# Moving the MLP's sums from VectorE to ScalarE and GpSimd, and fixing the order of the DMA and GpSimd queues

## Chip, core and metric

The kernel runs on one core of a Trainium2 chip. The metric is the device time in microseconds of one execution. The engines are called by the names that the profile uses: PE (TensorE; PEld is its weight load), DVE (VectorE), ACT (ScalarE), POOL (GpSimd) and SP (SyncE, which here only issues DMAs). Each engine takes its own instructions strictly in order; between engines an instruction waits for semaphores.

## What is computed

An attention block and a token-mixing MLP work on the same input and are mixed by a gate per token. S = 2048 tokens, D = 640 channels, H = 32 heads of 20, F = 1728, all float32:

```python
g = _sigmoid((x * gate_w).sum(-1, keepdims=True))
# a: attention
q, k, v = qkv[0], qkv[1], qkv[2]
scores = jnp.einsum("bhqd,bhkd->bhqk", q, k) * (Dh ** -0.5)
p = _softmax(scores, axis=-1)
o = jnp.einsum("bhqk,bhkd->bhqd", p, v)      # then @ wo
# b: MLP over the token axis
h = _layernorm(x, axis=-1)
u = _gelu(jnp.einsum("bsd,sf->bdf", h, w1) + b1)
y = jnp.einsum("bdf,fs->bds", u, w2) + b2    # transposed back
return g * a + (1 - g) * b
```

## The kernel before

**Precision.** Most products are made from numbers split into a high and a low part (`hi_lo`, L36): the high part is a rounded copy, the low part the difference. A product then takes three matmuls (high x high, high x low, low x high). In the MLP each matmul over 128 rows is cut in two halves of 64 rows that go to two accumulators side by side (`pair64`, L43); the two halves have to be summed afterwards. In this text they are `ps[0]` and `ps[1]`.

**Stages, in order of time.**

1. Projections (to about 220 us): units of q and k (`qk_unit`, L189) of 128 rows by 512 tokens, each of 15 matmuls, ACT writing the high part, DVE the low part, and SP storing both to q_d and k_d; v in between. In the last 24 units (L373) the first half of the channels is also normalised (`h_norm`, L314, POOL) and split (`h_split`, L318, ACT and POOL), the first four weight blocks are loaded (`w_raw`, L338) and split (`w_split`, L348), and the operands of the first pair of heads are loaded (`base_stack`, L114).
2. The MLP (about 220 to 745 us): `mlp` (L446) is a generator whose steps are one `pair64` each; 2592 steps. For each half d of the channels it makes 14 tiles u (48 steps each, one of them 32) and then 16 tiles y (40 steps each). Weights come in blocks of 128x512 (`w_need`, L364): loaded nine blocks ahead by SP, split four blocks ahead, high part on ACT, low part on POOL. A block feeds 12 steps, which are 24 matmuls.
3. Beside the MLP, scores: `s_tiles` (L136) makes a 128x512 tile of scores by one matmul and takes its row maxima by one DVE reduction (L148). The maxima of each query are needed later, to make the exponentials safe. 736 of the 2048 tiles are made here (S_AHEAD, L493), two at a time, spread evenly over the steps (L509); the others in the loop. After 64 tiles (half a pair of heads) the partial maxima are closed: a reduction, a negation, a split into high and low, a transposition (L151 to L157, all on DVE) and a store to m_d (L158).
4. The attention loop (about 745 to 1840 us): 16 pairs of heads times 32 iterations. An iteration makes four tiles of transposed scores (`st_op`, L640), four exponentials on ACT (L646), the four products with v for the iteration before (`pv_flush`, L580), and up to three of the remaining 1312 score tiles. The maxima enter the transposed scores as two extra rows of the operand (`load_m`, L120).
5. The output projection (from about 1840 us), which also adds the MLP's y, stored in between to y_d.

**Order.** PE's instructions run as the program lists them over the whole kernel, ACT's and DVE's from L212 to the end of the loop. POOL's and SP's are arranged by the scheduler of the framework, from its own estimates of durations, so a load may come earlier or later in its queue than the program has it. `settle` (L400) carries out evacuation steps a number of MLP steps after they were registered in `soon`.

**What the change touches.** `u_evac` (L408): ACT copies `ps[0]` to SBUF (L410), five steps later DVE adds `ps[1]` to it (L411), at step 10 follow gelu (L419) and the split. The tile FF has 64 rows in each half, so its two halves of rows are also swapped by DMAs and added on POOL (`u_swap`, L422). `y_evac` (L435): ACT scales and shifts `ps[0]` (L438), five steps later DVE adds the scaled `ps[1]` (L441) and SP stores the tile to y_d (L442). `h_norm` (L314) for the second half runs on POOL during the y tiles of the first half. `load_stack` (L96) issues 12 loads for a pair of heads on SP (14 with the rows of ones), for the first pair at unit 19, for pair p + 1 when pair p starts (`start_ahead`, L496); when pair 4 starts, the stack of the loop's first pair, its maxima and its v follow. The iteration of the loop takes its score tiles at L649 to L654.

Of the kernel before, what the change touches and what calls it, by code (L numbers as in the profile page):

```python
# [13 lines left out]
P = 128  # L14
# [14 lines left out]
def gated_mix(ctx, tc, xT, x, wqk, wv0, wv1, wo, w1, w1t, b1, w2, b2, out):  # L29
# [66 lines left out]
    def load_stack(p, ks, qs, full):  # L96
        for j in range(2):
            r0 = 64 * j
            h = 2 * p + j
            rows = slice(DH * h, DH * h + DH)  # L100
            kf = ks.bitcast(F32)
            nc.sync.dma_start(kf[r0: r0 + DH, :], k_d[0, rows, :])
            nc.sync.dma_start(kf[r0 + DH: r0 + 2 * DH, :], k_d[0, rows, :])
            nc.sync.dma_start(kf[r0 + 2 * DH: r0 + 3 * DH, :], k_d[1, rows, :])
            if full:
                nc.sync.dma_start(kf[r0 + 3 * DH: r0 + 3 * DH + 2, :], ones)
            for i in range(2):
                qf = qs[i].bitcast(F32)
                cols = slice(i * (S // 2), (i + 1) * (S // 2))
                nc.sync.dma_start(qf[r0: r0 + DH, :], q_d[0, rows, cols])  # L110
                nc.sync.dma_start(qf[r0 + DH: r0 + 2 * DH, :], q_d[1, rows, cols])
                nc.sync.dma_start(qf[r0 + 2 * DH: r0 + 3 * DH, :], q_d[0, rows, cols])

    def base_stack(p, full):  # L114
        ks = k8([P, S], F32R, f"ks{p}_{full}")
        qs = [q4([P, S // 2], F32R, f"qs{p}_{full}_{i}") for i in range(2)]
        load_stack(p, ks, qs, full)
        return ks, qs
# [16 lines left out]

    def s_tiles(p):  # L136
        for half in range(2):
            mx = cp.tile([P, 4, 2, 8], F32, tag="mx", bufs=2, name=f"mx{p}_{half}")
            for t in range(8):
                for kc in range(4):  # L140
                    for j in (1, 0):
                        def f(j=j, kc=kc, t=t):
                            ks, qs = s_src[p]
                            ps = s_tile([P, 512], f"s{p}_{half}_{t}_{j}_{kc}")
                            r = slice(64 * j, 64 * j + 3 * DH)
                            nc.tensor.matmul(ps, qs[half][r, t * P:(t + 1) * P], ks[r, kc * 512:(kc + 1) * 512],  # L146
                                             start=True, stop=True)
                            nc.vector.tensor_reduce(mx[:, kc, j, t: t + 1], ps, axis=AX.X, op=OP.max)  # L148
                        yield f
            mm = cp.tile([P, 16], F32, tag="mm", bufs=2, name=f"mm{p}_{half}")  # L150
            nc.vector.tensor_reduce(mm, mx.rearrange("p k j t -> p (j t) k"), axis=AX.X, op=OP.max)  # L151
            mc = cp.tile([P, 32], F32R, tag="mc", bufs=2, name=f"mc{p}_{half}")
            mt = cp.tile([P, 32], F32, tag="mt", bufs=2, name=f"mt{p}_{half}")
            nc.vector.tensor_scalar_mul(mc[:, :16], mm, -1.0)
            nc.vector.scalar_tensor_tensor(mc[:, 16:], mm, -1.0, mc[:, :16].bitcast(F32),
                                           op0=OP.mult, op1=OP.subtract)
            nc.vector.transpose(mt, mc.bitcast(F32))  # L157
            m_queue[0].dma_start(m_d[p, half], mt)  # L158
# [7 lines left out]
    m_queue = [nc.sync]  # L166
# [136 lines left out]

    hps = ExitStack()
# [9 lines left out]
    def h_norm(d, t):  # L314
        xm = xms[d, t]
        nc.gpsimd.tensor_scalar(xm, xm, negm[:, t:t + 1], rstd[:, t:t + 1], op0=OP.add, op1=OP.mult)
# [21 lines left out]
    def w_raw(k):  # L338
# [6 lines left out]
        nc.sync.dma_start(raw[:, :n, :m], src)  # L345
# [62 lines left out]
    def u_evac(f, d, ps, gh, gl):  # L408
        xg = gp.tile([P, HALF], F32, tag="xg", bufs=3, name=f"xg{d}_{f}")
        nc.scalar.activation(xg, ps[0], AF.Copy)  # L410
        soon.append([5, lambda: nc.vector.tensor_add(xg, ps[1], xg)])  # L411
# [10 lines left out]
    def u_swap(d, xg):  # L422
# [3 lines left out]
        nc.gpsimd.tensor_add(xg, xg, sw)  # L426
# [8 lines left out]
    def y_evac(t, d, ps):  # L435
        ty = hp.tile([P, HALF], F32, tag="ty", bufs=3, name=f"ty{d}_{t}")
        c = slice(t, t + 1)
        nc.scalar.activation(ty, ps[0], AF.Identity, bias=b2o[:, c], scale=omg[:, c])  # L438

        def rest():  # L440
            nc.vector.scalar_tensor_tensor(ty, ps[1], omg[:, c], ty, op0=OP.mult, op1=OP.add)  # L441
# [54 lines left out]
    def start_ahead(p):  # L496
        if 1 <= p + 1 < 6:
# [9 lines left out]
    for n, _ in enumerate(steps):  # L507
        settle()
        while done + 2 <= S_AHEAD and done < S_AHEAD * (n + 1) / STEPS:  # L509
            for _ in range(2):  # L510
                next(stream)()
            done += 2
    settle(True)
    while done < S_AHEAD:
        next(stream)()
# [19 lines left out]
    m_queue[0] = nc.gpsimd  # L535
# [85 lines left out]
    for p in range(NP):  # L621
# [3 lines left out]
        for it in range(32):  # L625
# [23 lines left out]
            due = min((p * 32 + it + 1) * LEFT // (NP * 32 - 38) + 1, LEFT)  # L649
            take = min(due - given, 3)  # L650
            for n in range(4):
                st_op((n + turn) % 2, n // 2, s_tile if n == 0 and take < 3 else st_tile)
                if n < take:
                    next(stream)()  # L654
            given += take
            if take and given == LEFT:
                next(stream, None)
# [83 lines left out]
```

## Time and profile before

| | us |
|---|---|
| median of 3 runs | 1918.32 |
| lowest and highest | 1918.08, 1920.92 |
| the profiled execution, whole | 1924.69 |
| its span in the profile | 1922.9 |

The profiled execution is another one than the three runs; it is 6.4 us above their median, and 1.8 us of it lie outside the span. Busy shares over the span are 98% for PE, 76% for DVE, 69% for ACT and 29% for POOL. They are averages over stages of quite different kinds, so the tables by stretch of time are read with them. A PE that is shown busy may still be slower than it could be, since ends of matmuls are modelled; the number of matmuls that start in a stretch is the surer measure. In a wait row stands the engine that waited, then the one that it waited for.

### The profile page before, as it was taken

The numbers are of one execution on the slowest core, as the hardware profiler recorded it, in microseconds if no ns is written. First come the engines' busy times: TensorE is split into PE (matmuls) and PEld (weight loads), VectorE is DVE, ScalarE is ACT, GpSimd is POOL, SyncE is SP. The second block draws the span as 40 slices with busy tenths as digits, with TensorE's granted clock in tenths as the row PEclk, the third lists the DMA queues.
The fourth block names the chain that finished last, engine by engine and source line by source line (L and its number), as shares of the span: only waits on it lengthen the run. The fifth ranks groups of instructions, "written<-read, shape, count | busy, mean of one in ns | idle before, by whom it ended". The sixth has DMA issues, their size and how long they took to land. (4 is left out here: it accounts for less than half of the span.)

```text
span 1922.9 us, 39183 instructions
## 1 busy us (share of the span) xinstructions
PE 1878.7 (98%) x14978; PEld 1162.0 (60%) x14978; DVE 1463.1 (76%) x2465; ACT 1335.4 (69%) x2595; POOL 557.5 (29%) x731
## 2 busy tenths in 40 slices
PE   9999889999999999999999999999999999999998
PEld 7998788998999996333333333333333333333378
DVE  4202388999999997888888888888888888886127
ACT  4253233343443335999999999999999999999930
POOL 1024266667776562210110101001220012111210
PEclk9999899999999998999999999999999999999999
DMA  8467775556655563315040404231542134211263
GB/s 282 139 198 220 208 180 153 148 162 175 171 141 142 163 177 93 80 40 113 7 97 12 99 16 89 53 84 24 107 101 69 32 76 99 48 34 52 70 217 134
DMA packets 153742, 216.63 MB, mean 113 GB/s; under 512 B 66783, under 2 KB 92991, under 8 KB 149647
## 3 DMA queue, kind: packets, MB, share of 16 engines
q1 hardware_dynamic: 136336, 186.96, 36.6%
q0 software_dynamic: 13472, 18.63, 4.3%
q10 hardware_dynamic: 3744, 8.52, 1.3%
q8 instruction: 118, 1.93, 0.5%
q14 instruction: 72, 0.58, 0.1%
HBM read 165.43 MB, written 48.25 MB: 111 GB/s over the span
## 5 line engine op out<-in xcount | busy, mean ns | idle before, releaser
L148 DVE TENSOR_REDUCE mx<-s 128x1 f32<-128x512 f32 x2048 | 1283.5, 683 | 168.8 <-PE s L146 149.5
L646 ACT ACTIVATE p<-st 128x512 f32<-128x512 f32 x2048 | 1050.8, 620 | 41.1 <-PE s L146 14.7
L643 PEld LDWEIGHTS st<-qs_True,ks_True 62*128 62x128 f32 x2048 | 326.5, 185 | 476.0 <-ACT p L646 229.8
L643 PE MATMUL st<-qs_True,ks_True 62*128 62x512 f32 x2048 | 606.5, 424 | 1.2 <-ACT p L646 0.8
L586 PE MATMUL pv<-p,v 128*32 128x512 f32 x4096 | 550.1, 606 | 0.0
L146 PE MATMUL s<-sk,sq 60*128 60x512 f32 x1280 | 442.2, 440 | 2.6 <-DVE mx L148 2.6
L41 POOL TENSOR_TENSOR wl<-wr,wh 128x512 fp32r<-128x512 f32 x228 | 271.8, 1215 | 117.4 <-ACT wh L38 100.2
L146 PE MATMUL s<-ks_False,qs_False 60*128 60x512 f32 x768 | 253.3, 411 | 11.7 <-DVE mx L148 11.7
L573 POOL DMA_DIRECT2D o_d<-oev x128 | 66.5, 519 | 611.4 <-DVE oev L567 593.3
L38 ACT ACTIVATE wh<-wr 128x512 fp32r<-128x512 f32 (+2 forms) x246 | 139.9, 594 | 137.0 <-PE y L46 50.4
L146 PEld LDWEIGHTS s<-sk,sq 60*128 60x128 f32 x1280 | 208.5, 184 | 21.6 <-DVE mx L148 12.7
L46 PE MATMUL y<-gh,wh 64*128 64x320 f32 x896 | 208.6, 310 | 0.0
L46 PE MATMUL u<-hh,wh 64*128 64x320 f32 x864 | 199.7, 310 | 4.4 <-ACT wh L38 4.4
L46 PE MATMUL y<-gh,wl 64*128 64x320 f32 x832 | 200.5, 310 | 2.7 <-POOL wl L41 2.7
L46 PE MATMUL y<-gl,wh 64*128 64x320 f32 x832 | 202.6, 310 | 0.0
L46 PE MATMUL u<-hl,wh 64*128 64x320 f32 x864 | 199.1, 309 | 0.0
L46 PE MATMUL u<-hh,wl 64*128 64x320 f32 x800 | 188.1, 311 | 4.5 <-POOL wl L41 4.5
L586 PEld LDWEIGHTS pv<-p,v 128*32 128x32 f32 x4096 | 83.0, 108 | 173.8 <-issue 162.1
L46 PEld LDWEIGHTS y<-gh,wh 64*128 64x128 f32 x896 | 154.3, 187 | 0.4
L146 PEld LDWEIGHTS s<-ks_False,qs_False 60*128 60x128 f32 x768 | 138.3, 188 | 24.9 <-DVE mx L148 23.4
L46 PEld LDWEIGHTS u<-hh,wh 64*128 64x128 f32 x864 | 150.0, 188 | 4.8 <-ACT wh L38 4.6
L46 PEld LDWEIGHTS u<-hl,wh 64*128 64x128 f32 x864 | 150.8, 188 | 0.3
(112 smaller groups left out, 1837.4 us busy)
## 6 DMA issues: line engine op xcount, KB each, us to landing
wr<-in_w_dram SPq DMA_DIRECT2D x200, 256.0 KB
qs_True<-q_d SPq DMA_DIRECT2D x192, 80.0 KB
ks_True<-k_d SPq DMA_DIRECT2D x96, 160.0 KB
sk<-k_d SPq DMA_DIRECT2D x60, 160.0 KB
sq<-q_d SPq DMA_DIRECT2D x120, 80.0 KB
qs_False<-q_d SPq DMA_DIRECT2D x72, 80.0 KB
ks_False<-k_d SPq DMA_DIRECT2D x36, 160.0 KB
v_d<-vt SPq DMA_DIRECT2D x32, 168.0 KB
```

Of the source, the lines that this page charges most:

```text
L38: nc.scalar.activation(hi, src, AF.Copy)
L41: (lo_eng or nc.vector).tensor_sub(lo, src, hi.bitcast(F32))
L46: nc.tensor.matmul(ps[k], a[r], b[r], start=start, stop=stop)
L146: nc.tensor.matmul(ps, qs[half][r, t * P:(t + 1) * P], ks[r, kc * 512:(kc + 1) * 512], start=True, stop=True)
L148: nc.vector.tensor_reduce(mx[:, kc, j, t: t + 1], ps, axis=AX.X, op=OP.max)
L573: nc.gpsimd.dma_start(o_d[DH * h: DH * h + DH, cols], ev[r: r + DH, :])
L586: nc.tensor.matmul(pv[r: r + 32, :], v_tiles[p][:, kt, 10 * j: 10 * j + 32], pts[j, c], start=(kt == 0), stop=(kt == NT - 1))
L643: nc.tensor.matmul(ps, ks[r, kt * P:(kt + 1) * P], qs[qh][r, c * 512:(c + 1) * 512], start=True, stop=True)
L646: nc.scalar.activation(pt, ps, AF.Exp, scale=SCALE)
```

## The change

Six things are altered.

- **Sums.** In `u_evac` and `y_evac` ACT now reads both accumulators (`half_sum`, a second copy, scaled for y), and POOL adds the two in SBUF six steps later. Gelu comes at step 18 instead of 10; the y tile's store is issued by ACT at step 24. The sum with the swapped halves comes at step 30 instead of at once. The normalisation of the second half of the channels (`h_norm`) is two ACT operations instead of one on POOL.
- **Maxima.** A closing is cut in three: the reduction on DVE two tiles after the last tile of a half, negation and split on POOL, and eight tiles later the transposition on DVE. The store goes to POOL's queue, in the MLP another eight tiles later.
- **Order.** POOL and SP run as programmed from L304 to the end of the loop.
- **Queues.** SP is left with loads. The first four weight blocks and the first stack are issued by POOL; the stack follows unit 19 instead of preceding it, and the first splits come one or two units later.
- **The second stack** is loaded when 48 score tiles have been made.
- **The loop.** In an iteration with two score tiles these follow its first and third tile of transposed scores instead of its first and second, and the order of the heads within it alternates differently. All score tiles are done six iterations earlier (44 instead of 38 before the end).

The diff, shortened:

```diff
-    def load_stack(p, ks, qs, full):
+    def load_stack(p, ks, qs, full, eng=nc.sync):
...
+    s_close = []
+
+    def s_max(p, half, mx):
+        mm = cp.tile([P, 16], F32, tag="mm", bufs=2, name=f"mm{p}_{half}")
+        mc = cp.tile([P, 32], F32R, tag="mc", bufs=2, name=f"mc{p}_{half}")
+        nc.vector.tensor_reduce(mm, mx.rearrange("p k j t -> p (j t) k"), axis=AX.X, op=OP.max)
+        nc.gpsimd.tensor_scalar_mul(mm, mm, -1.0)
+        hi_lo(mc[:, :16], mc[:, 16:], mm, hi_eng=nc.gpsimd, lo_eng=nc.gpsimd)
+        s_close.append([8, lambda: s_store(p, half, mc)])
+
+    def s_store(p, half, mc):
+        mt = cp.tile([P, 32], F32, tag="mt", bufs=2, name=f"mt{p}_{half}")
+        nc.vector.transpose(mt, mc.bitcast(F32))
+        s_close.append([M_LAG[0], lambda: m_queue[0].dma_start(m_d[p, half], mt)])
+
+    M_LAG = [8]
+
+    def s_next():
+        next(stream)()
+        for e in list(s_close):
+            e[0] -= 1
+            if e[0] <= 0:
+                s_close.remove(e)
+                e[1]()
...
-            mm = cp.tile([P, 16], F32, tag="mm", bufs=2, name=f"mm{p}_{half}")
-            nc.vector.tensor_reduce(mm, mx.rearrange("p k j t -> p (j t) k"), axis=AX.X, op=OP.max)
-            mc = cp.tile([P, 32], F32R, tag="mc", bufs=2, name=f"mc{p}_{half}")
-            mt = cp.tile([P, 32], F32, tag="mt", bufs=2, name=f"mt{p}_{half}")
-            nc.vector.tensor_scalar_mul(mc[:, :16], mm, -1.0)
-            nc.vector.scalar_tensor_tensor(mc[:, 16:], mm, -1.0, mc[:, :16].bitcast(F32),
-                                           op0=OP.mult, op1=OP.subtract)
-            nc.vector.transpose(mt, mc.bitcast(F32))
-            m_queue[0].dma_start(m_d[p, half], mt)
+            s_close.append([2, lambda p=p, half=half, mx=mx: s_max(p, half, mx)])
...
-    m_queue = [nc.sync]
+    m_queue = [nc.gpsimd]
...
+    ordered.enter_context(tc.manual_schedule(engines={EG.Pool, EG.SP}))
...
         xm = xms[d, t]
+        if d:
+            nc.scalar.activation(xm, xm, AF.Identity, bias=negm[:, t:t + 1])
+            nc.scalar.activation(xm, xm, AF.Copy, scale=rstd[:, t:t + 1])
+            return
         nc.gpsimd.tensor_scalar(xm, xm, negm[:, t:t + 1], rstd[:, t:t + 1], op0=OP.add, op1=OP.mult)
...
-        nc.sync.dma_start(raw[:, :n, :m], src)
+        (nc.gpsimd if k < AHEAD else nc.sync).dma_start(raw[:, :n, :m], src)
...
-        if n == 19:
-            s_src[0] = base_stack(0, False)
...
-        if n in (18, 19):
-            w_split(n - 18)
-            w_raw(n - 16)
+        if n in (19, 20):
+            w_split(n - 19)
+            w_raw(n - 17)
         qk_unit(m, w[m], q)
-        if n in (20, 21):
-            w_split(n - 18)
+        if n == 19:
+            s_src[0] = base_stack(0, False, nc.gpsimd)
+        if n in (22, 23):
+            w_split(n - 20)
...
         nc.scalar.activation(xg, ps[0], AF.Copy)
-        soon.append([5, lambda: nc.vector.tensor_add(xg, ps[1], xg)])
+        x2 = half_sum(ps[1], 1.0)
+        soon.append([6, lambda: nc.gpsimd.tensor_add(xg, xg, x2)])
         if f == FF:
-            soon.append([6, lambda: u_swap(d, xg)])
+            soon.append([7, lambda: u_swap(d, xg)])
+            soon.append([30, lambda: nc.gpsimd.tensor_add(xg, xg, sws.pop())])
             soon.append([44, lambda: u_tail(f, d, xg, gh)])
         else:
-            soon.append([10, lambda: u_gelu(f, xg, gh, gl)])
+            soon.append([18, lambda: u_gelu(f, xg, gh, gl)])
+
+    def half_sum(ps, scale):
+        x2 = gp.tile([P, HALF], F32, tag="x2", bufs=2, name="x2")
+        nc.scalar.activation(x2, ps, AF.Copy, scale=scale)
+        return x2
...
         nc.scalar.activation(ty, ps[0], AF.Identity, bias=b2o[:, c], scale=omg[:, c])
+        x2 = half_sum(ps[1], omg[:, c])
 
         def rest():
-            nc.vector.scalar_tensor_tensor(ty, ps[1], omg[:, c], ty, op0=OP.mult, op1=OP.add)
-            nc.sync.dma_start(y_d[t * P:(t + 1) * P, d * HALF:(d + 1) * HALF], ty)
-
-        soon.append([5, rest])
+            nc.gpsimd.tensor_add(ty, ty, x2)
+
+        def store():
+            nc.scalar.dma_start(y_d[t * P:(t + 1) * P, d * HALF:(d + 1) * HALF], ty)
+
+        soon.append([6, rest])
+        soon.append([24, store])
...
-        if 1 <= p + 1 < 6:
+        if 2 <= p + 1 < 6:
             s_src[p + 1] = base_stack(p + 1, False)
...
+            if done == 48:
+                s_src[1] = base_stack(1, False)
...
-    m_queue[0] = nc.gpsimd
+    M_LAG[0] = 0
...
-            due = min((p * 32 + it + 1) * LEFT // (NP * 32 - 38) + 1, LEFT)
+            due = min((p * 32 + it + 1) * LEFT // (NP * 32 - 44) + 1, LEFT)
             take = min(due - given, 3)
             for n in range(4):
-                st_op((n + turn) % 2, n // 2, s_tile if n == 0 and take < 3 else st_tile)
-                if n < take:
-                    next(stream)()
+                j = n // 2 if take == 2 else n % 2
+                st_op((j + turn) % 2, n % 2 if take == 2 else n // 2, s_tile if n == 0 and take < 3 else st_tile)
+                if n < take if take != 2 else n % 2 == 0:
+                    s_next()
```

More of the change, by code (lines that the diff above doesn't have):

```diff
@@ L101, in load_stack @@
             kf = ks.bitcast(F32)
-            nc.sync.dma_start(kf[r0: r0 + DH, :], k_d[0, rows, :])
-            nc.sync.dma_start(kf[r0 + DH: r0 + 2 * DH, :], k_d[0, rows, :])
-            nc.sync.dma_start(kf[r0 + 2 * DH: r0 + 3 * DH, :], k_d[1, rows, :])
+            eng.dma_start(kf[r0: r0 + DH, :], k_d[0, rows, :])
+            eng.dma_start(kf[r0 + DH: r0 + 2 * DH, :], k_d[0, rows, :])
+            eng.dma_start(kf[r0 + 2 * DH: r0 + 3 * DH, :], k_d[1, rows, :])
             if full:
-                nc.sync.dma_start(kf[r0 + 3 * DH: r0 + 3 * DH + 2, :], ones)
+                eng.dma_start(kf[r0 + 3 * DH: r0 + 3 * DH + 2, :], ones)
             for i in range(2):
@@ L109, in load_stack, with base_stack @@
                 cols = slice(i * (S // 2), (i + 1) * (S // 2))
[L110 to L114, printed above, removed]
+                eng.dma_start(qf[r0: r0 + DH, :], q_d[0, rows, cols])
+                eng.dma_start(qf[r0 + DH: r0 + 2 * DH, :], q_d[1, rows, cols])
+                eng.dma_start(qf[r0 + 2 * DH: r0 + 3 * DH, :], q_d[0, rows, cols])
+    def base_stack(p, full, eng=nc.sync):
         ks = k8([P, S], F32R, f"ks{p}_{full}")
         qs = [q4([P, S // 2], F32R, f"qs{p}_{full}_{i}") for i in range(2)]
-        load_stack(p, ks, qs, full)
+        load_stack(p, ks, qs, full, eng)
         return ks, qs
@@ L134, in load_v, with s_finish @@
         nc.sync.dma_start(v_tiles[p], v_d[p // 8, :, :, c0: c0 + NPAIR].rearrange("t p c -> p t c"))
+    s_close = []
[18 more added lines that the diff above has]
+                e[1]()
+    def s_finish():
+        next(stream, None)
+        while s_close:
+            s_close.pop(0)[1]()
     def s_tiles(p):
@@ L410, in u_evac @@
         nc.scalar.activation(xg, ps[0], AF.Copy)
-        soon.append([5, lambda: nc.vector.tensor_add(xg, ps[1], xg)])
+        x2 = half_sum(ps[1], 1.0)
+        soon.append([6, lambda: nc.gpsimd.tensor_add(xg, xg, x2)])
         if f == FF:
-            soon.append([6, lambda: u_swap(d, xg)])
+            soon.append([7, lambda: u_swap(d, xg)])
+            soon.append([30, lambda: nc.gpsimd.tensor_add(xg, xg, sws.pop())])
             soon.append([44, lambda: u_tail(f, d, xg, gh)])
         else:
-            soon.append([10, lambda: u_gelu(f, xg, gh, gl)])
+            soon.append([18, lambda: u_gelu(f, xg, gh, gl)])
[3 more added lines that the diff above has]
+        return x2
+    sws = []
     def u_gelu(f, xg, gh, gl):
@@ L425, in u_swap @@
         nc.gpsimd.dma_start(sw[TL:], xg[:TL])
-        nc.gpsimd.tensor_add(xg, xg, sw)
+        sws.append(sw)
     def u_tail(f, d, xg, gh):
@@ L514, in gated_mix @@
     while done < S_AHEAD:
-        next(stream)()
+        s_next()
         done += 1
@@ L647, in st_op @@
                 pts[j, c] = pt
-            due = min((p * 32 + it + 1) * LEFT // (NP * 32 - 38) + 1, LEFT)
+            due = min((p * 32 + it + 1) * LEFT // (NP * 32 - 44) + 1, LEFT)
             take = min(due - given, 3)
             for n in range(4):
-                st_op((n + turn) % 2, n // 2, s_tile if n == 0 and take < 3 else st_tile)
-                if n < take:
-                    next(stream)()
+                j = n // 2 if take == 2 else n % 2
+                st_op((j + turn) % 2, n % 2 if take == 2 else n // 2, s_tile if n == 0 and take < 3 else st_tile)
+                if n < take if take != 2 else n % 2 == 0:
+                    s_next()
             given += take
             if take and given == LEFT:
-                next(stream, None)
+                s_finish()
             turn = (turn + take) % 2
```

## The prediction

> **What bounds the kernel now.** I read the page's slices first, to find stages, and then the windows of the stage that the change touches.
>
> ```profile
> span 1922.9 us, 39183 instructions
> PE   9999889999999999999999999999999999999998
> DVE  4202388999999997888888888888888888886127
> PEclk9999899999999998999999999999999999999999
> ```
>
> One digit is 48 us. PE is full nearly everywhere, so its share tells little. DVE has two levels: nines from about 240 to 740 us, where the MLP runs with the first 736 score tiles beside it, and eights in the attention loop. PEclk is an eight only at the two ends of the MLP stage. The change acts in that stage above all, so its windows come next (columns: stretch; busy time and instructions of PE, PEld, DVE, ACT, POOL; granted clock; DMA share; GB/s).
>
> ```profile
> core 0: us, PE busy (x) PEld busy (x) DVE busy (x) ACT busy (x) POOL busy (x), PEclk, DMA share, GB/s
> ...
> 215.00:740.00 525.00, 496.22 (x5913) 477.83 (x5913) 487.37 (x834) 192.53 (x370) 328.94 (x306) 0.97 0.58 159
> ...
> 220.00:230.00 10.00, 3.77 (x21) 3.15 (x22) 3.06 (x5) 2.31 (x4) 1.29 (x1) 0.67 0.83 274
> 230.00:240.00 10.00, 9.78 (x101) 9.43 (x101) 8.39 (x15) 2.05 (x4) 1.63 (x2) 0.82 0.63 190
> ...
> 250.00:260.00 10.00, 5.17 (x33) 4.00 (x31) 3.04 (x6) 3.75 (x8) 5.00 (x5) 0.70 0.82 221
> ...
> 420.00:430.00 10.00, 10.00 (x128) 9.77 (x126) 9.89 (x18) 3.70 (x7) 5.53 (x6) 1.00 0.49 147
> 555.00:565.00 10.00, 10.00 (x131) 10.00 (x129) 10.00 (x17) 3.82 (x8) 5.89 (x5) 1.00 0.64 170
> 720.00:730.00 10.00, 7.66 (x62) 7.66 (x64) 7.34 (x13) 0.63 (x1) 2.72 (x3) 0.66 0.25 74
> 760.00:1765.00 1005.00, 1002.39 (x6938) 392.29 (x6938) 852.29 (x1418) 967.17 (x1879) 157.46 (x295) 1.00 0.30 65
> ```
>
> The matmul counts are the measure here. Undisturbed, PE starts 128 to 131 matmuls in 10 us, so the 5913 of the stage need 451 to 462 us; it takes 525. **At least 63 us of this stage are lost time**, and DVE, with 487 us of work, could not have done it in much less than it took: two engines are near their limit at once. Four windows hold 23 us of the loss: 21 + 101 + 33 + 62 = 217 matmuls where 512 fit, (512 - 217) / 12.8 = 23. In each the granted clock falls to between 0.66 and 0.82 beside the gap, so an idle stretch of PE is paid for again afterwards.
>
> In the loop (760 to 1765 us) PE and ACT are busy 1002 and 967 of 1005 us, DVE 852. DVE has slack there on average, not in bursts. Now the waits of the MLP stage (engine, line, what it waited for: total us, times, longest), and after them groups of instructions (us busy, mean ns of one, idle before):
>
> ```profile
> PEld s L146 <- DVE mx L148: 23.4, 49, 2.8
> ACT wh L38 <- DMA wr<-in_w_dram: 23.2, 5, 9.7
> ACT evh L38 <- DMA q_d<-evh: 13.3, 1, 13.3
> PEld u L46 <- DVE evl L41: 5.7, 1, 5.7
> PEld u L46 <- POOL wl L41: 5.6, 3, 4.2
> PEld u L46 <- ACT wh L38: 4.6, 1, 4.6
> PEld y L46 <- POOL wl L41: 3.6, 4, 2.0
> ```
>
> PE waits 23.4 us for score maxima, and 5.7 + 5.6 + 4.6 + 3.6 = 19.5 us for operands that are late. The lateness starts in SP's queue: one store of q waits 13.3 us (this holds ACT, then DVE, then PE for 5.7), and weight loads hold ACT 23.2 us in five waits. SP had stack loads ahead of both.
>
> **The change part by part: the MLP stage.** What is moved, with its durations:
>
> ```profile
> L148 DVE TENSOR_REDUCE mx<-s 128x1 f32<-128x512 f32 x728 | 451.8, 683 | 17.4 <-PE s L146 14.7
> L41 POOL TENSOR_TENSOR wl<-wr,wh 128x512 fp32r<-128x512 f32 x228 | 271.8, 1215 | 117.4 <-ACT wh L38 100.2 <-DMA wr<-in_w_dram 14.0 <-DMA m_d<-mt 3.1
> L441 DVE SCALAR_TENSOR_TENSOR ty<-y,omg,ty 128x320 f32<-128x320 f32 x32 | 17.4, 542 | 0.7 <-ACT ty L438 0.7
> L411 DVE TENSOR_TENSOR xg<-u,xg 128x320 f32<-128x320 f32 x28 | 13.5, 482 | 6.9 <-ACT xg L410 6.9
> L438 ACT ACTIVATE ty<-y,b2o,omg 128x320 f32<-128x320 f32 x32 | 19.8, 619 | 91.8 <-PE y L46 79.7 <-PE s L146 12.0
> L410 ACT ACTIVATE xg<-u 128x320 f32<-128x320 f32 x28 | 12.2, 436 | 94.1 <-PE u L46 83.0 <-PE s L146 11.1
> L426 POOL TENSOR_TENSOR xg<-xg,sw 128x320 f32<-128x320 f32 x2 | 1.7, 870 | 6.1 <-DMA wr<-in_w_dram 3.8 <-DMA sw<-xg 2.3
> L316 POOL TENSOR_SCALAR xm<-xm,negm,rstd 128x320 f32<-128x320 f32 x32 | 19.5, 610 | 59.8 <-DMA xm<-in_x_dram 48.3 <-DMA qs_False<-q_d 4.0 <-PE y L46 4.0
> L154 DVE TENSOR_SCALAR mc<-mm 128x16 fp32r<-128x16 f32 x11 | 3.9, 359 | 0.4
> L155 DVE SCALAR_TENSOR_TENSOR mc<-mm,mc 128x16 fp32r<-128x16 f32 x11 | 4.4, 402 | 0.4
> L176 ACTq DMA_DIRECT2D wr<-in_wqk_dram x10: 334/335/450, 0.7 to 191.8; - x10
> ```
>
> DVE loses 60 sums (17.4 + 13.5 = 30.9 us) and the two middle steps of eleven closings of the maxima (3.9 + 4.4 = 8.3): 487 becomes 448 us, below PE's 462. So PE becomes the bound, with DVE just under it.
>
> ACT gains 28 copies of 0.436, 32 scaled copies of 0.619, 32 steps of the second half's normalisation (no row; between 0.436 and 0.619, I take the middle, 17 us) and 32 issues of y stores at 0.335: 12 + 20 + 17 + 11 = 60 us on 193. It stays near half busy, and its PSUM reads now come at once, so the accumulators are released earlier. I cost this at nothing; it is hidden behind PE as long as the hi splits keep their lead of four weight groups.
>
> POOL gains 60 additions of 0.870 (52 us), 11 issues of maxima stores (6 us at the 0.573 of the loop's, quoted below) and 33 operations on 128x16. No row shows those on POOL; they lie between nothing and the 0.610 of the 128x320 row above, up to 20 us; I take 7. It loses 16 normalisations (10 us): 329 + 55 = 384 us of some 484, 79%. The densest stretch is a y tile of the first half: three and a half weight splits, one addition, one split of h, about 4.3 + 0.9 + 0.9 = 6.1 us against the 40 x 2 + 11 = 91 matmuls of the tile, 7.1 us. It fits, with a seventh to spare.
>
> The queues. In program order SP no longer has y stores, m stores or the first stack ahead of weight loads; the first stack and four weight loads go to POOL, 16 issues at the 0.52 of L573 below, 8 us within the last seven projection units. The second stack moves from the stage's start to 48 score tiles in. So the 13.3 us store wait and the early weight waits lose their cause. What is late next: the first stack itself, which POOL issues behind a split, and whose 1.9 MB share the DMA engines with the q and k stores. I leave 3 us for PE there. At the fifth pair SP gets two stacks, m and v in one go ahead of weight loads, some 4.2 MB by their shapes; at the 221 to 274 GB/s of the busiest windows above that is 15 to 19 us, against a lead of nine groups of 24 matmuls, 17 us without the score tiles between: between nothing and 5 us lost, I take nothing.
>
> The sum for the stage: of the four windows' 23 us I take back 19. Of PE's 23.4 us for maxima, some 18 lie outside them, of which 14 go with the sums and the long closings. Of the late operands outside them and the clock behind those, 8. **41 us less**; 22 of the 63 stay.
>
> How long one closing in this stage is, and in the loop (timeline: start, us, idle before in brackets), with POOL's rows of the loop:
>
> ```profile
> 719.38 0.87 DVE L154 TENSOR_SCALAR mc<-mm 128x16 fp32r<-128x16 f32 x1
> 720.29 1.19 DVE L155 SCALAR_TENSOR_TENSOR mc<-mm,mc 128x16 fp32r<-128x16 f32 x1
> ```
> ```profile
> 872.75 0.26 DVE L151 TENSOR_REDUCE mm<-mx 128x16 f32<-128x64 f32 x1
> ...
> 873.47 0.21 DVE L157 STREAM_TRANSPOSE mt<-mc 128x32 f32<-128x32 f32 x1
> ...
> 876.49 2.79 ACT L646 ACTIVATE p<-st 128x512 f32<-128x512 f32 x5 [0.81 <-PE s L146]
> ```
> ```profile
> L158 POOL DMA_DIRECT2D m_d<-mt x21 | 12.0, 573 | 243.3 <-DVE mt L157 242.9 <-issue 0.2
> L573 POOL DMA_DIRECT2D o_d<-oev x116 | 60.3, 520 | 550.5 <-DVE oev L567 532.4 <-DVE mm L151 15.5 <-issue 2.6
> L40 POOL CAST woh<-wor 128x640 fp32r<-128x640 f32 x4 | 2.8, 712 | 24.8 <-DMA wor<-in_wo_dram 24.8
> ```
>
> **The loop.** A closing occupies DVE from 872.75 to 873.68, and ACT then sits 0.81 us; over 20 closings that is 16 us at most. After the change DVE is interrupted for 0.26, and eight tiles later for 0.21. With 15% of slack in 852 of 1005 us such pieces fit between score tiles: 12 us less. The new order of the score tiles in iterations with two, and their end six iterations earlier, keep every instruction; no row prices them. ACT idles only 1005 - 967 = 38 us in the loop, 16 of it for closings, so at most 22 can be won, and as much lost; I take 1 us lost, since at the end six more iterations run without score tiles.
>
> **The seam.** The last y tile now needs, before ACT may start the exponentials, its second copy (0.619), POOL's addition (0.870) and a store's issue (0.335): 2 us more.
>
> Sum: -41 - 12 + 1 + 2 = -50. The profiled execution took 1924.7 us (span 1922.9), so 1874.7; the median of the runs lies 6.4 lower, at 1918.3, so **1868**.
>
> **Rivals.**
>
> *POOL becomes the bound of the MLP.* The additions cost 0.870 on POOL and 0.482 on DVE. If POOL's work stretches by 1.3 under the fuller load, a y tile of the first half takes 7.9 instead of 7.1 us: 16 x 0.8 = 13 us lost, and as much again in clock and late splits elsewhere, -24 in all: 1894. For it: 79% mean load in strict program order. Against it: POOL idled 117 us before its splits, and DVE's own two-input sums are gone. The Trainium skill, GPSIMD Engine Reference, section Engine selection, speaks against this change: elementwise work with two inputs belongs on VectorE, GpSimd being about half as fast. The trace agrees on the ratio, 870 to 482 ns; by that rule the change would give away 52 us of POOL for 31 of DVE and come out near this rival, while I hold that it counts only where POOL is last.
>
> *DVE waits for POOL at each closing: slower.* The transposition on DVE now waits for three POOL operations. In front of them on POOL may stand eight store issues (4 us) or a load of wo with its wait (6 us, 24.8 / 4) and its splits. Behind the transposition queue all score maxima, and PE behind them. DVE has eight score tiles, some 5 us in the MLP and 6 in the loop, before it asks. If POOL is later than that by 2.5 us on average, 32 closings lose 80 us: 1868 + 80 = 1948. Against it: 4 us of issues are under 6, and the maxima's operations mostly come before a wo load.
>
> *The sums were hidden anyway.* If PE's 23.4 us were paid for by the loads' order alone and the new order of POOL and SP costs as much as it saves, only the loop's 12 us and little else are left, or nothing: 1905 to 1918.
>
> **How the numbers follow.** Forecast 66%, POOL's bound 16%, slower 8%, hidden 10% (of this a third is no change). Faster by over 0.2%, about what a measurement of this kernel can tell: 0.89; within it 0.03; slower 0.08. The low end takes the whole 63 us of the MLP and 16 of the loop less the seam, 1918 - 77 = 1841, which needs everything to fit; I stop at 1847. The high end takes in POOL's bound and the better half of the hidden case: 1906.
>
> **What would show it.** Right: the MLP stage some 40 us shorter, near 125 matmuls in most 10 us windows, the clock near 1.00 from 230 us on, PE's wait for maxima under 10 us, POOL near 380 us busy, no 0.8 us gaps in the loop at closings. Wrong: DVE's transposition waiting for POOL, weight splits ending PE's waits in y tiles, a dark window at the first stack or the fifth pair, or a stage that loses as much in other windows.

## Result: half the gain that was forecast

| | before | after |
|---|---|---|
| median of 4 runs, us | 1919.62 | 1893.64 |
| lowest to highest | 1918.08 to 1927.25 | 1889.89 to 1898.79 |
| profiled execution | 1924.69 | 1889.89 |

The ratio is 0.9866, with a 95% interval of 0.9847 to 0.9886: 26 us less, where 50 were forecast. Only about half of the forecast gain came, so a step of the sum is wrong.

The stages of the two profiled executions, from the first and last matmuls of each kind (us):

| stage | before | after | difference | forecast |
|---|---|---|---|---|
| up to the first u matmul | 219.7 | 219.6 | -0.1 | 0 |
| MLP, first u to last y matmul | 525.4 | 503.7 | -21.7 | -41 |
| seam, to the first product with v | 4.8 | 6.6 | +1.8 | +2 |
| loop, first to last product with v | 1090.2 | 1077.4 | -12.8 | -11 |
| rest | 82.9 | 80.9 | -2.0 | 0 |
| sum | 1922.9 | 1888.1 | -34.8 | -50 |

Seam and loop came as forecast. **The MLP stage alone is 19 us short.** The page of the changed kernel (its span, and PE, DVE, POOL and the granted clock in 40 slices of 47 us):

```profile
span 1888.1 us, 39235 instructions
PE   9999999999996999999999999999999999999998
DVE  4202399999995998888888888888888878884037
POOL 1014578888884772111111111121331121211210
PEclk9999999999998999999999999999999999999999
```

The six and the five in one slice, in the middle of a row of nines, are the answer: PE and DVE, and the clock with them, fall at about 580 us. The windows there, with one of the usual ones ahead of them:

```profile
420.00:430.00 10.00, 10.00 (x130) 9.97 (x129) 10.00 (x17) 5.61 (x12) 9.40 (x10) 1.00 0.69 195
...
570.00:580.00 10.00, 8.06 (x102) 7.80 (x98) 8.97 (x15) 0.68 (x2) 2.73 (x3) 1.00 0.61 154
580.00:590.00 10.00, 0.00 (x0) 0.00 (x0) 0.00 (x0) 0.00 (x0) 0.00 (x0) 0.62 0.40 75
590.00:600.00 10.00, 4.25 (x30) 3.72 (x32) 1.29 (x2) 4.28 (x9) 4.68 (x5) 0.52 0.93 262
```

130 matmuls per 10 us, as the windows count them, is the full pace; these three windows hold 132 instead of 390, a loss of 20 us. For 10 us no compute engine does anything, while the DMA engines are at 0.40. PE then returns at half the clock. The waits of the stage say for what (engine, line, waited for: us, times, longest):

```profile
ACT wh L38 <- DMA wr<-in_w_dram: 40.0, 8, 23.9
...
PEld u L46 <- ACT wh L38: 17.4, 1, 17.4
PE u L46 <- ACT wh L38: 17.2, 1, 17.2
...
PEld y L46 <- POOL wl L41: 2.9, 4, 1.1
...
DVE mt L148 <- POOL mc L41: 1.7, 1, 1.7
...
PEld s L176 <- DVE mx L178: 0.6, 1, 0.6
```

PE waits 17.2 us for ACT's high part, ACT for one weight load, 23.9 us long. Most of what had held PE before is gone: for maxima its weight loads (PEld) wait 0.6 us where it had been 23.4. Why the load is late stands in SP's queue (start, us until the last of a group ended):

```profile
546.00 9.04 SPq L372 DMA_DIRECT2D wr<-in_w_dram  x5
555.14 0.32 SPq L102 DMA_DIRECT2D ks_False<-k_d  x1
...
570.35 0.27 SPq L102 DMA_DIRECT2D ks_True<-k_d  x1
...
583.66 5.62 SPq L127 DMA_DIRECT2D qs_True<-m_d  x8
589.32 0.45 SPq L134 DMA_DIRECT2D v<-v_d  x1
589.88 10.37 SPq L372 DMA_DIRECT2D wr<-in_w_dram  x11
```

From 555.1 to 589.8 us SP issues what the start of the fifth pair asks for: a stack (18 loads), the loop's first stack (20), eight loads of maxima and v. For 34.7 us no weight block is asked for. PE runs 23 us on what is loaded and split, then stops at 578.1 us; it goes on at 595.3 us, 5.4 us after the first new weight load is issued. In the kernel before, where the scheduler arranged SP's queue, weight loads stood between the loads of the loop's first stack:

```profile
549.23 0.32 SPq L110 DMA_DIRECT2D qs_True<-q_d  x1
...
551.94 1.58 SPq L345 DMA_DIRECT2D wr<-in_w_dram  x2
553.57 0.36 SPq L112 DMA_DIRECT2D qs_True<-q_d  x1
...
554.43 0.36 SPq L345 DMA_DIRECT2D wr<-in_w_dram  x1
```

### The profile page after: what moved, and what is told of

Read it like the earlier page. It is cut to its first block, busy times and chain, and to the rows that moved or that the text cites. A ratio compares the mean times of both kernels' runs of the same rounds, so it can differ in the third digit from the quotient of the medians.

```text
span 1888.1 us, 39235 instructions
## 1 busy us (share of the span) xinstructions
PE 1847.1 (98%) x14978; PEld 1141.0 (60%) x14978; DVE 1427.7 (76%) x2341; ACT 1364.0 (72%) x2687; POOL 638.8 (34%) x904
## 4 chain that ended last, share of the span: by engine, by line
PE 72%; DMA 3%; DVE 1%; issue 1%; SPq 1%; POOL 0%; ACT 0%; DVEq 0%; POOLq 0%; ACTq 0%
PE pv L628 27%; PE st L685 23%; PE s L176 9%; PE y L46 7%; PE u L46 4%; PE a L718 1%; DMA qs_False<-q_d 1%; PE b L718 1%; DMA sq<-q_d 1%; DMA ks_True<-k_d 1%; SPq L127 0%; DMA oy<-y_d 0%; DMA o_d<-oev 0%; DMA wr<-in_w_dram 0%; DMA r_d<-rl 0%
## 5 line engine op out<-in xcount | busy, mean ns | idle before, releaser
L685 PEld LDWEIGHTS st<-qs_True,ks_True 62*128 62x128 f32 x2048 | 319.2, 186 | 490.6 <-ACT p L688 274.8
L685 PE MATMUL st<-qs_True,ks_True 62*128 62x512 f32 x2048 | 598.7, 429 | 5.2 <-ACT p L688 2.8
L176 PE MATMUL s<-ks_False,qs_False 60*128 60x512 f32 x768 | 217.7, 399 | 3.9 <-DMA qs_False<-q_d 3.7
L46 PE MATMUL u<-hh,wh 64*128 64x320 f32 x864 | 160.3, 308 | 17.3 <-ACT wh L38 17.2
L46 PE MATMUL u<-hl,wh 64*128 64x320 f32 x864 | 160.1, 307 | 0.0
L46 PE MATMUL u<-hh,wl 64*128 64x320 f32 x800 | 150.6, 309 | 2.3 <-POOL wl L41 2.3
L46 PEld LDWEIGHTS y<-gh,wl 64*128 64x128 f32 x832 | 143.1, 184 | 3.2 <-POOL wl L41 2.9
L46 PEld LDWEIGHTS y<-gl,wh 64*128 64x128 f32 x832 | 143.2, 184 | 0.1
L176 PEld LDWEIGHTS s<-ks_False,qs_False 60*128 60x128 f32 x768 | 120.6, 186 | 4.6 <-issue 3.9
```

The costliest lines, as they stand in the source:

```text
L46: nc.tensor.matmul(ps[k], a[r], b[r], start=start, stop=stop)
L685: nc.tensor.matmul(ps, ks[r, kt * P:(kt + 1) * P], qs[qh][r, c * 512:(c + 1) * 512], start=True, stop=True)
```

## Experiments

Three things were asked: whether this burst is the whole of the shortfall, what each part of the change is worth, and what the order of POOL and SP does. Times are medians; the changed kernel is at 1893.6, and at 1890.7 when measured a second time. "Loses" and "gains" are against these two.

### The burst taken apart

```diff
-        if p == 4:
-            st_src[0] = base_stack(0, True)
-            load_m(0, st_src[0][1])
-            load_v(0)
...
+            if done == 576:
+                st_src[0] = base_stack(0, True)
+            if done == 640:
+                load_m(0, st_src[0][1])
+                load_v(0)
```

> The changed kernel, with the loop's first stack loaded when 576 score tiles are done and its maxima and v at 640, instead of all of them at 512 together with pair 5's stack. Theory (the burst): SP issues 47 loads in one go there, the weight loads stand behind them, PE idles 17 us and then runs at a granted clock near 0.5; without the burst both go, 26 us of matmuls come back, and the time is near 1893.6 - 25 = 1868 us, with no window of the MLP under 100 matmuls in 10 us after 300 us. Rival (the volume): the same bytes must still pass, so a gap of 5 us or more opens at one of the new places, and the time stays within 8 us of 1893.6.

Measured 1878.1 us, ratio 0.9779 (0.9757 to 0.9800). The gap is gone, and the MLP takes 484.8 us: 40.6 less than before the change, where 41 was forecast. The stage is 19 us shorter than in the change, and 13 to 16 us of that reach the median: in the profiled executions the loop is 1.3 us and the rest 2.7 us longer. The expected 25 was too much to begin with; the missing matmuls of the three windows are worth 20. Two windows of this run (columns as above):

```profile
580.00:590.00 10.00, 10.00 (x132) 10.00 (x130) 9.88 (x17) 5.27 (x12) 8.44 (x9) 1.00 0.37 107
...
610.00:620.00 10.00, 8.73 (x107) 8.04 (x105) 7.81 (x13) 3.64 (x7) 5.12 (x6) 1.00 0.92 266
```

The moved stack is issued from 595.6 to 610 us, and behind it a small loss is left: 107 matmuls instead of 130, about 2 us instead of 19. No gap of 1 us or more opens there, so the rival (the volume) falls.

### A smaller burst

```diff
         if p == 4:
             st_src[0] = base_stack(0, True)
-            load_m(0, st_src[0][1])
-            load_v(0)
...
+            if done == 640:
+                load_m(0, st_src[0][1])
+                load_v(0)
```

> The changed kernel with two stacks still together at the fifth pair, but the loop's first maxima and v at 640 score tiles: 38 loads ahead of the weight loads instead of 47. In the changed kernel those nine take SP from 583.7 to 589.9 us. Theory (the gap is the length of the queue ahead of the weight loads): PE's gap of 17.2 us shrinks by about 6, to 10 to 12 us: 1883 to 1889 us. Rival (a gap opens once a threshold is passed, by buffers or engines that are full): gap within 2 us of 17 or of nothing.

Measured 1884.0 us, 0.9803 (0.9772 to 0.9834). SP's queue and PE's wait:

```profile
583.18 0.27 SPq L112 DMA_DIRECT2D qs_True<-q_d  x1
584.12 15.92 SPq L372 DMA_DIRECT2D wr<-in_w_dram  x15
```
```profile
PEld u L46 <- ACT wh L38: 9.9, 1, 9.9
```

The weight loads are asked for 5.8 us earlier (584.1 instead of 589.9), and PE's gap shrinks from 17.2 to 9.6 us (14.7 in the second run of the change, so by 5 to 8). It follows the length of the queue ahead of the weight loads, as the theory has it.

### The sums back on DVE

```diff
-        x2 = half_sum(ps[1], 1.0)
-        soon.append([6, lambda: nc.gpsimd.tensor_add(xg, xg, x2)])
+        soon.append([6, lambda: nc.vector.tensor_add(xg, ps[1], xg)])
...
-        x2 = half_sum(ps[1], omg[:, c])
...
-            nc.gpsimd.tensor_add(ty, ty, x2)
+            nc.vector.scalar_tensor_tensor(ty, ps[1], omg[:, c], ty, op0=OP.mult, op1=OP.add)
```

> The changed kernel, with the 60 sums back on DVE (one operation on PSUM and SBUF, six steps after the tile) and no second copy on ACT. Theory (DVE was as near its limit as PE): DVE's work in the MLP is 31 us more, about 480 us against PE's 460, so PE waits for maxima again, 12 to 25 us in all: 1906 to 1919 us, PE's wait for the maxima's reductions over 10 us, 126 to 129 matmuls in a usual 10 us window. Rival (the sums were hidden): within 5 us of 1893.6, since only the long closings and the late loads had held PE.

Measured 1896.5 us, 0.9891 (0.9857 to 0.9925): 3 us more than the first median of the changed kernel, 6 more than the second. The rival (within 5 us) is met by the first and just missed by the second; the theory's 12 to 25 us falls. The 31 us of DVE work were nearly all hidden in this kernel. The matmuls of a long stretch without gaps (290 us) show the rest:

```profile
285.00:575.00 290.00, 289.99 (x3584) 282.73 (x3583) 287.94 (x493) 133.30 (x262) 208.61 (x210) 1.00 0.58 163
```

DVE is 288 of 290 us busy and PE makes 3584 matmuls; the changed kernel makes 3621 in the same stretch, and the version with single loads (below) 3671, or 127 in 10 us. (A window of 10 us also counts the 3 or 4 matmuls that reach over its edge, so its 130 is the same pace.) With three score accumulators PE stayed within 3% of that although DVE was at its limit.

### The closings back on DVE

```diff
-            s_close.append([2, lambda p=p, half=half, mx=mx: s_max(p, half, mx)])
...
+            nc.vector.tensor_reduce(mm, mx.rearrange("p k j t -> p (j t) k"), axis=AX.X, op=OP.max)
...
+            nc.vector.tensor_scalar_mul(mc[:, :16], mm, -1.0)
+            nc.vector.scalar_tensor_tensor(mc[:, 16:], mm, -1.0, mc[:, :16].bitcast(F32),
+                                           op0=OP.mult, op1=OP.subtract)
+            s_store(p, half, mc)
```

> The changed kernel, with each closing of the maxima again one block of four operations on DVE; only the store stays where the change put it. Theory: in the loop most of 20 closings cost 0.8 us again (12 to 16 us), in the MLP eleven cost 0.3 to 1 us more each because the two middle steps wait for POOL: 15 to 25 us in all, 1908 to 1919. Rival: DVE has the slack now, so a closing costs nothing in the MLP and the loop loses under 6 us: under 1900.

Measured 1920.0 us, ratio 0.9999 (0.9979 to 1.0020): **26 us more, as much as the whole change brings**, and just above the theory's range. The runs of this kernel lie between 1912.7 and 1931.1, and the profiled one, at 1925.5, is above the median: in it the MLP takes 17 us more (520.7 instead of 503.7) and the loop 17.5 (1094.9 instead of 1077.4). In the loop one gap of 5.2 us is not a closing's: PE waits for maxima whose loads stand behind a stack in SP's queue.

```profile
885.20 0.76 PE L691 MATMUL st<-qs_True,ks_True 62*128 62x512 f32 x1 [5.23 <-DMA qs_True<-m_d]
```

One closing in the MLP (DVE, then POOL at the same time), the two middle steps in the stage, and PE's wait:

```profile
439.07 1.14 DVE L183 TENSOR_SCALAR mc<-mm 128x16 fp32r<-128x16 f32 x1
440.24 1.19 DVE L184 SCALAR_TENSOR_TENSOR mc<-mm,mc 128x16 fp32r<-128x16 f32 x1
```
```profile
437.63 3.77 POOL L41 TENSOR_TENSOR wl<-wr,wh 128x512 fp32r<-128x512 f32 x3
```
```profile
L184 DVE SCALAR_TENSOR_TENSOR mc<-mm,mc 128x16 fp32r<-128x16 f32 x11 | 7.2, 655 | 0.4
L183 DVE TENSOR_SCALAR mc<-mm 128x16 fp32r<-128x16 f32 x11 | 6.6, 602 | 0.4
```
```profile
PEld s L176 <- DVE mx L178: 17.4, 11, 2.8
```

Each of the two steps ends with one of POOL's splits of 1.2 us. In this kernel, where POOL is fuller, they take 602 and 655 ns on average, in the kernel before 359 and 402. The 17.4 us of PE's weight loads are eleven waits, as many as there are closings. The Trainium skill, SBUF — State Buffer, section Who interferes with whom, has the rule: a DVE operation in a 2-port mode, which a tensor_scalar can enter, and GpSimd exclude each other for the whole instruction, whoever issues first going first, and a DVE operation with two SBUF inputs contends with a GpSimd instruction that reads SBUF. The two rows, 1.14 and 1.19 us beside POOL's splits, fit it; in which mode the tensor_scalar ran, no trace shows.

### The closings on DVE, but apart

```diff
-        nc.gpsimd.tensor_scalar_mul(mm, mm, -1.0)
-        hi_lo(mc[:, :16], mc[:, 16:], mm, hi_eng=nc.gpsimd, lo_eng=nc.gpsimd)
+        s_close.append([2, lambda: nc.vector.tensor_scalar_mul(mc[:, :16], mm, -1.0)])
+        s_close.append([5, lambda: nc.vector.scalar_tensor_tensor(mc[:, 16:], mm, -1.0, mc[:, :16].bitcast(F32),
+                                                                  op0=OP.mult, op1=OP.subtract)])
```

> The changed kernel, with all four operations of a closing on DVE, but apart: the reduction after 2 score tiles, the negation 2 later, the low part 3 after that, the transposition another 3 later. Theory (DVE's middle steps wait for POOL): in the MLP each still waits up to a microsecond for POOL's running operation, 6 to 12 us over eleven closings, nothing in the loop where POOL is idle: 1899 to 1906 us, with mean times of these two steps over 300 ns in the MLP. Rival (the block of four is too long, whatever makes it long): apart they fit between the score tiles: within 4 us of 1893.6.

Measured 1895.4 us, 0.9869 (0.9845 to 0.9893): within 2 us of the first median, 5 of the second. The steps still wait for POOL:

```profile
L142 DVE TENSOR_SCALAR mc<-mm 128x16 fp32r<-128x16 f32 x11 | 5.2, 476 | 0.0
L143 DVE SCALAR_TENSOR_TENSOR mc<-mm,mc 128x16 fp32r<-128x16 f32 x11 | 4.1, 376 | 0.0
```

So both halves of the question are answered: the wait for POOL is there, 476 and 376 ns, and apart it costs 2 to 5 us instead of 26. What held PE was 2 to 3 us of DVE at a stretch, longer than the three accumulators bridged. That POOL does the middle steps is worth 2 to 5 us; that the block is cut in pieces is worth the rest.

### The closings alone, in the kernel before

The functions `s_max`, `s_store`, `s_next` and `s_finish` of the change, without the lag of the store, in the kernel before; sums and order as they were.

> The kernel before, with the closings in three parts as in the changed kernel and nothing else (sums on DVE, order by the scheduler). Theory (the closings are the larger part of the gain, as the run with closings on DVE says): 20 to 28 us less than before, 1891 to 1899. Rival (in the kernel before the late loads and the sums hold PE anyway): only the loop's 10 to 14 us: 1904 to 1909.

Measured 1915.1 us, 0.9964 (0.9948 to 0.9981): neither. The MLP gains 16.5 us (508.9), as the theory says; the loop loses 8. One wait takes the gain back (POOL, then DVE):

```profile
770.85 0.71 POOL L40 CAST woh<-wor 128x640 fp32r<-128x640 f32 x1 [7.72 <-DMA wor<-in_wo_dram]
...
776.70 0.71 POOL L40 CAST woh<-wor 128x640 fp32r<-128x640 f32 x1 [2.68 <-DMA wor<-in_wo_dram]
777.50 1.52 POOL L41 TENSOR_TENSOR wol<-wor,woh 128x640 fp32r<-128x640 f32 x1
779.00 0.25 POOL L142 TENSOR_SCALAR mm<-mm 128x16 f32<-128x16 f32 x1
```
```profile
779.85 0.21 DVE L148 STREAM_TRANSPOSE mt<-mc 128x32 f32<-128x32 f32 x1 [15.15 <-POOL mc L41]
```

The scheduler has put two blocks of wo ahead of the closing's steps in POOL's queue, hundreds of microseconds early (with the fixed order of the change POOL splits wo between 1250 and 1540 us). POOL waits for their loads, DVE waits 15.2 us for POOL, PE 13.7 for DVE. This is the mechanism of the prediction's second rival, a load of wo with its wait in front of the closing, though once and not at each closing. With the order fixed, as in the change, it does not happen.

### The change without the fixed order

```diff
-    ordered.enter_context(tc.manual_schedule(engines={EG.Pool, EG.SP}))
```

> The changed kernel without the one line that fixes the order of POOL and SP: the scheduler arranges both as before. Theory (order makes the burst): weight loads are mixed into the stack loads again, so the gap at the fifth pair shrinks to under 5 us, worth 15 us, but loads and POOL's work come early or late elsewhere as in the kernel before, costing 5 to 15 of it: 1880 to 1893 us. Rival (the loads themselves): the 47 loads still stand together and the gap stays over 10 us: 1890 to 1900.

Measured 1896.1 us, 0.9877 (0.9855 to 0.9899): inside the rival's range and outside the theory's. Yet the mechanism is the theory's in the MLP: 492.6 us, no gap over 1 us at the fifth pair, 7.5 us lost in two gaps at 232 and 283 us. But the loop is 17 us longer, by the same wait as above:

```profile
766.20 0.21 DVE L148 STREAM_TRANSPOSE mt<-mc 128x32 f32<-128x32 f32 x1 [16.63 <-POOL mc L41]
```

So the fixed order saves one wait of 16 us in POOL's queue and makes one of 17 in SP's.

### Order, queues and loop alone

The changed kernel with two of the edits above: the sums and the closings back on DVE.

> The changed kernel with sums and closings both on DVE: what is left of the change is the order of POOL and SP, the queues, the moved loads and the loop's order. Theory (these bring about 19 us by loads that are no longer late and lose 17 to 26 us at the burst): no gain, 1915 to 1925 us, with a gap over 10 us at the fifth pair and PE waiting over 20 us for maxima in the MLP. Rival (the order brings a gain of its own): under 1908.

Measured 1917.1 us, 0.9987 (0.9971 to 1.0003): no gain, as the theory says.

```profile
PEld s L176 <- DVE mx L178: 24.4, 52, 2.6
PEld u L46 <- ACT wh L38: 17.0, 2, 16.5
```

The two large waits of PE's weight loads stand side by side here: one that the closings and the sums make, one that the burst makes. Beside the run with the sums alone on DVE (1896.5) the closings are worth 21 us, a check on the 26 above. Beside the run with the closings alone on DVE (1920.0) the sums are worth nothing: as long as the closings hold PE, moving them does not help.

### The loop's order as before

The expression for the take and the inner loop of the kernel before, with 38 in place of 44, in the changed kernel.

> The changed kernel, with the loop's order and its end of the score tiles as before. The prediction counted this edit as 1 us lost; by that the time is 1893 us within 2. Theory after seeing the trace: iterations with two score tiles went from 2.07 to 1.94 us and the iteration after each from 2.08 to 2.14, so some 6 to 9 us are lost here: 1900 to 1903 us.

Measured 1898.0 us, 0.9883 (0.9859 to 0.9907): 4 and 7 us more than the two medians, below the theory's bounds. But by the traces only 2 to 3 us of that lie in the loop, which the edit touches (1080.0 us, against 1077.4 and 1078.3 in the two runs of the change); 5 to 6 lie in the MLP, which it leaves alone, where the gaps at 220 us and at the fifth pair are longer here (6.5 and 18.3 us). The prediction had put the edit at 1 us lost; it gains 2 to 3 us.

### The unaltered change again

> The changed kernel unaltered, on the same chip as the others of this call. Its first profile was its fastest run and the profile of before one of that kernel's slower ones. If that was scatter of the runs: the median again near 1893 us, the gap at the fifth pair again 14 to 18 us, and a profiled execution near the median.

Measured 1890.7 us, 0.9846 (0.9810 to 0.9882), gap 14.7 us, the profiled execution at 1888.3. The runs of this kernel spread over 10 us, and the profiled one was at the low end both times.

### Single loads

Every stack load of the MLP after the first stack, and the loop's first maxima, go into a list, and one is issued for every two score tiles; in the loop the maxima are loaded at iteration 20.

```diff
+    class Drip:
+        def dma_start(self, dst, src):
+            drips.append(lambda: nc.sync.dma_start(dst, src))
...
-            s_src[p + 1] = base_stack(p + 1, False)
+            s_src[p + 1] = base_stack(p + 1, False, dr)
...
+            if done == 576:
+                st_src[0] = base_stack(0, True, dr)
+            if done == 640:
+                load_m(0, st_src[0][1], dr)
+            if done == 704:
+                load_v(0)
+            drop()
...
-                if it == 26:
+                if it == 20:
                     load_m(p + 1, st_src[p + 1][1])
```

> The changed kernel, with every stack load of the MLP but the first stack's put into the SP queue one at a time, one for every two score tiles, the loop's first stack from 576 score tiles on, its maxima from 640, its v at 704; and in the loop the maxima's loads at iteration 20 instead of 26. Theory (what is left of the lost matmuls after 260 us are bursts of stack loads, and 2 us waits for maxima in the loop are too): 6 to 10 us under the run that only took the fifth pair's burst apart (1878): 1868 to 1872, no window of the MLP under 115 matmuls after 240 us. Rival (what is left is the load of ACT and POOL in the y tiles): the low windows near 410 and 610 us stay, and the time is within 3 us of 1878.

Measured **1865.3 us, 0.9718 (0.9694 to 0.9741)**: the fastest of all, a little under the expected. The MLP takes 482.1 us. Cut at full tens, no window of 10 us after 280 us holds fewer than 128 matmuls; the low ones that are left stand at the stage's start (46 from 220 us on) and here:

```profile
270.00:280.00 10.00, 7.47 (x82) 6.32 (x81) 6.47 (x12) 3.73 (x9) 8.16 (x12) 1.00 0.75 179
```

The loop takes 1072.7 us, 5 less than in the change. There, four times a stack of 18 loads had stood ahead of the maxima, and once PE waited for it, 2.2 us (SP, then PE):

```profile
1533.11 0.27 SPq L112 DMA_DIRECT2D sq<-q_d  x1
1534.97 5.99 SPq L127 DMA_DIRECT2D qs_True<-m_d  x8
```
```profile
1540.65 0.47 PE L685 MATMUL st<-qs_True,ks_True 62*128 62x512 f32 x1 [2.19 <-DMA qs_True<-m_d]
```

What the other 3 us of the loop come from was not traced. The rival (low windows near 410 and 610 us stay) falls: 130 and 131 matmuls there.

### Single loads with the sums on DVE

The sums' edit above, in the version with single loads.

> The version with single stack loads and early maxima (1865 us), with the sums on DVE. Theory (the sums were nearly hidden, and what they cost is PE's small waits for maxima): 3 to 6 us more, 1868 to 1871, 122 to 125 matmuls in a usual 10 us window of the MLP instead of 130. Rival (beside the burst the sums' cost was masked; with clean loads DVE's 31 us are the bound): 12 us or more, over 1877.

Measured 1873.7 us, 0.9752 (0.9727 to 0.9778): 8.4 us more than with the sums on ACT and POOL, between theory and rival. All of it lies in the MLP (490.9 instead of 482.1 us), where PE's weight loads wait 11.2 us for maxima. The sums are worth 8 us once little else stops PE; beside the burst, 3 to 6.

## Why the prediction was wrong, step by step

**The step that failed** is the fifth pair's loads: "at the 221 to 274 GB/s of the busiest windows above that is 15 to 19 us, against a lead of nine groups of 24 matmuls ...: between nothing and 5 us lost, I take nothing." The mechanism was named, its size was not seen. The loads held the queue for 34.7 us, in which the DMA engines moved 4.3 MB, 124 GB/s (last column):

```profile
555.14:589.88 34.74, 22.92 (x291) 22.66 (x287) 23.72 (x40) 7.24 (x15) 15.02 (x17) 0.89 0.57 124
```

The rate was taken from windows full of large weight loads and q and k stores. These loads are others: 36 of the 47 have 20 rows each, and eight have 4 KB in runs of 128 bytes. That their shape makes them slow is likely, but no run tried it. The lead was 23 us, more than the 17 (without score tiles) of the prediction. The queue was 12 us longer than the lead, and 5 us more passed from the first weight load to PE's next matmul, which the prediction had not counted: 17 us of idle PE. With the slow clock behind it that is the 19 us by which the MLP fell short; without the burst the stage took 484.8 us, with a smaller one 496.3. The count of loads was also wrong: a stack is 18 loads, 20 with the rows of ones, not 12 and 14.

**The second miss is the reference.** The sum was made against a profiled execution of 1924.7 us, and 6.4 us were taken off for the median. The changed kernel's own profiled execution lay 3.7 us under its median. Against profiles the miss is 15 us (1874.7 and 1889.9), which the burst accounts for: 19 us of the MLP, less 4 that loop and rest gained beyond the forecast. The other 10 us, between profile and median, are scatter of runs, 9 us wide in either kernel. A constant offset between profile and median was not something that one execution could show.

**Right in its sum, wrong in its parts:** of the 23.4 us of waits for maxima nearly all went, and the MLP without the burst came out 40.6 us shorter for 41. That the sum fits so well is in part luck. The 23.4 us are waits of PEld; PE's own row was half as long:

```profile
PE s L146 <- DVE mx L148: 11.7, 13, 2.5
```

The prediction put 14 us on closings and sums and 27 on loads and the clock behind them. By the runs the closings bring 17 us of the MLP (put back in the change: 520.7 for 503.7; taken out in the kernel before: 525.4 to 508.9) and the sums 5. By subtraction that leaves some 19 for the loads that are no longer late, an estimate. And the credit went to DVE's load falling to 448 us, below PE's 462. It did not: DVE is busy for 467 us of the stage (third pair of numbers in the first line below). The reductions take 464.2 us of it, 451.8 before (eight more of them lie in this window), at the same 0.68 us each. PE's 462 was read a little low itself: windows of 10 us count the matmuls at their edges twice, and at 127 in 10 us the stage's 5913 need 467 us, so 58 us of it were lost time and not 63.

```profile
215.00:723.00 508.00, 482.58 (x5973) 473.65 (x5974) 467.12 (x760) 227.05 (x461) 389.19 (x405) 0.98 0.58 160
```
```profile
L178 DVE TENSOR_REDUCE mx<-s 128x1 f32<-128x512 f32 x736 | 464.2, 685 | 33.0 <-PE s L176 29.0
```

**Right:** the loop's closings (12 us forecast; the loop is 12.8 shorter in all, of which the order of iterations with two score tiles, put at 1 us lost, is 2 to 3 gained); the seam; POOL at 389 us busy for 384 forecast, without becoming the bound. So the first rival fell. The advice of the Trainium skill, GPSIMD Engine Reference, section Engine selection, would have kept the sums on DVE; here, where POOL was not last, moving them gained 3 to 8 us once the closings were out of the way. The second rival did not occur in the change, where DVE waited for POOL once, 1.7 us; its mechanism did in both runs without a fixed order. The third rival was right about the sums, which were nearly hidden (3 to 6 us), and wrong about the time, since the closings were not. The early stall at 220 us was 3.7 us, for 3 forecast.

**What stays open:** the closings cost 26 us when put back on DVE in the changed kernel and bring only 7 when taken out in the kernel before (ratio 0.9964). The 15 us wait of DVE for POOL explains most of that difference; the rest, some 4 us, is within the scatter of these kernels' runs and was not traced. Some of the 26 us may be the 5.2 us gap in the loop and the slow clock behind it (0.69 from 880 to 890 us), where the maxima's loads met a stack in SP's queue; whether the closings on DVE bring that about was not tried. Nor was the rate of the small loads tried alone.

## What to carry to other kernels

Two engines near their limit do not tell which work to move: 31 us of DVE work were worth nothing to 8, and 0.9 to 3 us at a stretch, twenty and eleven times, were worth 21 to 26. Look for the longest time in which the engine that empties the accumulators does something else, and cut it below what the buffers bridge.

A fixed program order takes away the scheduler's surprises and puts the program's own bursts in their place. Where all loads of a queue are issued in order, count the time from the first issue of a burst to the next urgent load, by rows of loads of the same shape, and compare it with the lead; or issue the burst one load at a time.

## What the runs showed of the hardware

The granted clock fell beside gaps that were not long. A gap of 2.5 us in the kernel before stood in a window at 0.66, and gaps of 2.0 us and less left it at 1.00 there. In the run with the closings on DVE, though, a gap of 1.65 us at 485.5 us stood in a window at 0.83, and one of 2.00 us at 353.8 us in a window at 1.00:

```profile
350.00:360.00 10.00, 8.00 (x102) 7.74 (x100) 9.79 (x17) 4.03 (x9) 6.17 (x7) 1.00 0.47 130
...
485.00:495.00 10.00, 8.35 (x85) 8.01 (x84) 8.55 (x15) 2.34 (x5) 7.13 (x7) 0.83 0.66 140
```

So between 1.65 and 2.0 us the length of a gap alone did not decide. The 17.2 us gap of the changed kernel reached into a window at 0.52, with 30 matmuls in it. Small operations on POOL (128x16) took 0.20 to 0.25 us, nearer to nothing than to the 0.61 that had bounded them.
